# Reordering the start-up of a fused FFT and feed-forward kernel: splits ahead of the activation, a fold ahead of the copies, conversions one to three units earlier

## The chip, the cores and the metric

The kernel runs on one core of a Trainium2 chip. The metric is the device time of one execution in microseconds (us), the median over several runs. The kernel uses TensorE (PE, matrix products), VectorE (DVE), ScalarE (ACT), GpSimd (POOL) and the DMA queues, mostly SyncE's (SP).

## The reference, cut to what matters

```
X = np.fft.fft(np.fft.fft(x, axis=1), axis=2).real       # x: 8 x 3008 x 256, float32
h = X.reshape(24064, 256) @ w_in                          # w_in: 256 x 2048
g = np.where(h >= 1, h, np.where(h <= -1, 0, (h + 1) ** 2 / 4))
out = g @ w_out                                           # w_out: 2048 x 256
```

The weights arrive as 64-bit floats. The kernel turns them into float32 itself.

## The kernel before, in words

**Two kinds of work.** For each of the 8 batches the sequence transform is done as 64 x 47 (stage 1: eight pieces `p0` to `p7` per batch; then a small "nyquist" product `p8`; then stage 2: six pieces `p9` to `p14`, each of which makes half of one of three column chunks). The hidden-dimension transform is folded into `w_in`. What is left is cut into 384 *units*, one for each batch, column chunk `k` (three) and slice `f` of 128 of the 2048 hidden features. Batch 0 goes first through `f` 0 to 3 of the three chunks (units 0 to 11), then through `f` 4 to 15 of each (units 12 to 23, 24 to 35, 36 to 47).

**One unit.** `gemm1(i)` (L410) makes six products into two `uv` banks (three banks in all, L417), then DVE forms `us` (L422) and the two halves of `h` (L424, L425), then ACT makes `a` (Relu at L428, Square at L429). `activate(i)` (L432) joins `a` and `h` on DVE. For units under 24 the result `g` (L437) is multiplied in float32 (`wo32`, eight product records); from unit 24 on DVE's `h` (L440) is split by ACT into `gh` (L443) and by POOL into `gl` (L446), and `gemm2` makes twelve faster products. `gemm2` (L455) adds into four accumulator banks; at the end of a group of slices DVE and ACT empty two banks each (L489, L487; L485 where a stored part is added).

**The order of work at the start is written by hand.** `START` (L67) and `STEPS` (L72) name small steps by a letter and a number. In unit `i` of the main loop (L572) come, in this order: `gemm1(i)`, `activate(i-1)`, `gemm2` of an earlier unit, and then the steps of `STEPS[i]`. `gemm2` begins at unit 2, and is left out in the two units of `SKIP` (8 and 13), so that it then runs four units behind. `pin()` (L559) fixes each engine's order of issue to the program's order up to unit 23; after that the framework's scheduler orders. The steps that matter here:

- `a`, `b`, `c`, `d` of a weight block n convert it: `a` takes its fields (two DVE operations, L208 and L209), `b` is three on ACT (L214 to L216), `c` joins them (two on DVE, L221 and L222), `d` scales on POOL (L236; on DVE as `v`). Blocks 2, 3, 6, 7, 10, 11, 14 and 15 are parts of `w_out`, the others of `w_in`.
- `F`, `f` fold a half or a slice of `w_in` on PE and copy its high part on ACT (L279, L287); `s` makes its low part on DVE (L300, L305); `R`, `r`, `e`, `E` move a correction row `delta` (L291, L268).
- `u` and `O` make the high (ACT, L247) and low (DVE, L251) parts of `w_out` that units from 24 on need. The tile of the low parts lies on the raw blocks 6 to 9.
- `x`, `L` load the input of batch 0 and 1 (SP); `y`, `g` fold it (DVE or POOL, L137), and `Y` folds it on POOL behind DVE's last step.
- `p` issues the products of a piece; `t`, `w` copy stage 1 out of its bank (`w`: half on ACT at L339, half on DVE at L337); `q` splits a stage-2 piece into a high part on ACT (L174) and a low part on DVE (L175). `p8` also copies a row on ACT (L357) and stores it by a DMA from ACT's queue (L360); `n` (L367) waits for that store and reads it back over all partitions.
- `i`, `j` are products that only keep PE busy; `G` is `activate`.

**Banks.** The first 12 transform banks of batch 0 use the four accumulator banks in turn (L168). Those after share one bank, `fft`, so that `p12` must wait until `q11` has read `p11` out. Fold products 3 and 5 use a `uv` bank (L275).

**Later batches.** While a batch runs through its units, the next one's transform pieces are spread between them; for batch 1 this starts at unit `NEXT` = 23 (L575).

Of the kernel before, what the change touches and what calls it, by code (L numbers as in the profile page):

```python
# [26 lines left out]
NCHUNK = 3  # L27
NFT = FF // P
LAG = 4
SKIP = (8, 13)  # L30
EVICT_AHEAD = 150

C_ORDER = [*range(1, 8), 0, *range(8, NC)]
# [5 lines left out]
def _constants():  # L39
# [25 lines left out]


START = (  # L67
# [3 lines left out]
)  # L71
STEPS = {  # L72
    0: "p11 c2 d2 G0 i4",
    1: "q11 p12 a3 b3 i4",
    2: "a4 c3 d3 b4 q12",
    3: "c4 d4",
    4: "p13 a5 q13 b5",
    5: "p14 q14",
# [1 line left out]
    7: "a8 b8",  # L80
    8: "f2 f3 c8 d8 s2 s3 r1",
    9: "a9 b9",
    11: "a6 c9 d9 b6",
    12: "a12 b12",
    13: "f4 f5 c6 d6 s4 s5 r2",
    14: "a13 c12 d12",
    15: "b13",
    16: "a7 c13 d13 b7",
    17: "f6 c7 d7 s6 u0 L0 L1",
    18: "f7 a10 s7 b10 r3 u1",  # L90
    19: "a11 c10 d10 b11",
    20: "a14 O0 Y0 b14 u2 L2",
    21: "O1 c11 d11 u3",
    22: "a15 O2 Y1 b15 L3 u4",
    23: "O3 c14 d14 u5",
    24: "O4 c15 d15 u6",
    25: "O5 u7",
    26: "O6 O7",
}

RAW = {0: "gh", 1: "gh", 2: "woh", 3: "woh", 4: "woh", 5: "woh", 6: "wol", 7: "wol", 8: "wol", 9: "wol"}
# [6 lines left out]
NATIVE = 24  # L108
PINNED = 24
SPARE = (3, 5)  # L110
NEXT = 23


@with_exitstack
def fft_ffn_kernel(ctx: ExitStack, tc: tile.TileContext, x, cst, w_in, w_out, out):
# [16 lines left out]
    def fold_x(b, q, engine=None):  # L132

        t = xt.pop((b, q))
        engine = engine or nc.gpsimd
        y = sb.tile([96, CH], F32, tag="y", name=f"y_{b}_{q}", bufs=3)
        first = engine.tensor_tensor(y, t[:96, 0], t[:96, 1], op=ALU.add)  # L137
        yt[b, q] = y
        if q == 0:
            y = sb.tile([96, NA], F32, tag="yd", name=f"yd_{b}", bufs=1)  # L140
            engine.tensor_tensor(y, t[:96, 0, :NA], t[:96, 1, :NA], op=ALU.subtract)
            yt[b, "d"] = y
        return first.ins

    def fold_x_behind_vector(q):
        last = [ins for ins in traced if ins.engine == mybir.EngineType.DVE][-1]
        sync = mybir.DependencyInfo(mybir.DependencyClass.Sync, mybir.DependencyReason.DATA)
        tc.add_manual_dep(fold_x(1, q), last.name, sync, reason="beside VectorE's next steps")
# [158 lines left out]
    s1, s2 = {}, {}  # L307

    def stage1_sums(b, q):
        if q == 0:  # L310
            zt[b] = sb.tile([P, NC, P + 1], F32, tag="z", name=f"z_{b}", bufs=1)
        y = yt[b, q]
        bank = fft_bank(b, f"s1_{b}_{q}")
        pt = bank[:, : GPC * 96].rearrange("p (i n) -> p i n", i=GPC)
        for i in range(GPC):
            nc.tensor.matmul(pt[:, i], y[:, i * P : (i + 1) * P], bm[:96, :], start=True, stop=True)  # L316
        if q == 0:
            pd = bank[:NA, GPC * 96 : GPC * 96 + 2 * NC]
            nc.tensor.matmul(pd, yt[b, "d"], bm[:96, : 2 * NC], start=True, stop=True)
        s1[b, q] = bank  # L320
# [6 lines left out]
    def stage1_copy(b, q, vector=False):  # L327
        z, bank = zt[b], s1[b, q]
        if q == 0 and b:
            stage1_last(b, bank)  # L330
        pt = bank[:, : GPC * 96].rearrange("p (i n) -> p i n", i=GPC)
        for h in range(2):
            for m in range(2):
                src = pt[h * NA : (h + 1) * NA].rearrange("p i (t m c) -> p m c (i t)", t=2, m=2)[:, m]
                dst = z[m * NA : (m + 1) * NA, :, (2 * q + h) * 8 : (2 * q + h + 1) * 8]
                if vector and h:
                    ins = nc.vector.tensor_copy(dst, src)  # L337
                else:
                    ins = nc.scalar.activation(dst, src, AF.Copy)  # L339
                if b == 0:  # L340
                    if q:
                        tc.declare_no_dep(ins.ins, group="z", reason="other columns")
                    tc.add_to_no_dep_group("z", ins.ins)
    def stage1(b, q):
        for p in range(q, min(q + 2, XC)):
            if (b, p) in xt and (b, p) not in yt:
                fold_x(b, p)
        stage1_sums(b, q)
        stage1_copy(b, q)

# [43 lines left out]
    def fft_pieces(b):  # L394
        pieces = []
        for q in range(XC):
            pieces.append((4, lambda q=q: stage1(b, q)))
        pieces.append((2, lambda: nyquist(b)))
        for h in range(NC // 4):
            pieces.append((4, lambda h=h: stage2(b, h)))  # L400
        return pieces
# [8 lines left out]
    def gemm1(i):  # L410
        b, k, f = units[i]
        n = WIDTH[k]
        hi, lo = pq[b, k]
        cols = slice(f * P, (f + 1) * P)
        uv = []
        for m in range(2):
            t = ps.tile([P, CH], F32, tag="uv", name=f"uv_{i}_{m}", bufs=3)  # L417
            for j, (w, r) in enumerate(((wh, hi), (wl, hi), (wh, lo))):
                nc.tensor.matmul(t[:, :n], w[m][:, cols], r[:, m, :n], start=(j == 0), stop=(j == 2))  # L419
            uv.append(t[:, :n])  # L420
        us = sb.tile([P, CH], F32, tag="us", name=f"us_{i}", bufs=2)[:, :n]
        nc.vector.scalar_tensor_tensor(us, nyb[b, k][:, :n], delta[:, f : f + 1], uv[0], op0=ALU.mult, op1=ALU.add)  # L422
        h = sb.tile([P, 2, CH], F32, tag="h", name=f"h_{i}", bufs=3)[:, :, :n]
        nc.vector.tensor_tensor(h[:, 0], us, uv[1], op=ALU.subtract)  # L424
        nc.vector.tensor_tensor(h[:, 1], us, uv[1], op=ALU.add)  # L425
        a = sb.tile([P, 2, CH], F32, tag="a", name=f"a_{i}", bufs=3)[:, :, :n]

        nc.scalar.activation(a, h, AF.Relu, bias=half, scale=0.5)  # L428
        nc.scalar.activation(a, a, AF.Square)  # L429
        fronts[i] = h, a  # L430

    def activate(i):  # L432
        n = WIDTH[units[i][1]]
        h, a = fronts.pop(i)
        if i < NATIVE:
            g = sb.tile([P, 2, CH], F32, tag="gh", name=f"g_{i}", bufs=4)[:, :, :n]
            nc.vector.scalar_tensor_tensor(g, a, 1.0, h, op0=ALU.min, op1=ALU.max)  # L437
            acts[i] = (g,)
            return
        nc.vector.scalar_tensor_tensor(h, a, 1.0, h, op0=ALU.min, op1=ALU.max)  # L440
        gh = sb.tile([P, 2, CH], F32R, tag="gh", name=f"gh_{i}", bufs=4)[:, :, :n]
        gl = sb.tile([P, 2, CH], F32R, tag="gl", name=f"gl_{i}", bufs=4)[:, :, :n]
        nc.scalar.activation(gh, h, AF.Copy)  # L443
        acts[i] = gh, gl
        for sg in range(2):
            nc.gpsimd.tensor_tensor(gl[:, sg], h[:, sg], gh[:, sg].bitcast(F32), op=ALU.subtract)  # L446
# [61 lines left out]
    n1 = XC  # L508
# [43 lines left out]
    def run_steps(names):  # L552
        for s in names.split():
            steps[s[0]](int(s[1:] or 0))
# [17 lines left out]
    for i in range(n_units + LAG):  # L572
        if i < n_units:
            b, r = divmod(i, per)
            r0 = NEXT if b == 0 else 0  # L575
            if r == r0:
                pending = fft_pieces(b + 1) if b + 1 < NB else []
                done, total = 0, sum(w for w, _ in pending)
                if pending and b:
                    for q in range(4):  # L580
                        load_x(b + 1, q)
            gemm1(i)
            if b == 0 and units[i][2] == NFT - 2:
                load_parts(units[i][1])
            if 1 < i <= PINNED:
                activate(i - 1)
            if i >= PINNED:
                activate(i)
        first, _, then = STEPS.get(i, "").rpartition("|")
        run_steps(first)  # L590
        if 2 <= i < PINNED and i not in SKIP:
            gemm2(second)
# [72 lines left out]
```

## Time and profile before

| | |
|---|---|
| three runs | 1768.59, 1768.91 (median), 1779.52 us |
| the profiled execution's own time | 1767.59 us |
| its span | 1765.8 us |
| mean granted TensorE clock | 0.996 |
| PE busy | 1735.6 us (98%) |
| DVE busy | 1421.5 us (80%) |
| ACT busy | 1334.8 us (76%) |
| POOL busy | 1164.2 us (66%) |

The profile is of one execution. Each engine's instructions can be listed in order of time: start, duration, engine, source line, operation, output and input tiles, count, and in brackets how long the engine had been idle before it and what it waited for. Matmuls overlap at their ends, so a PE that looks busy can still lose a few tenths of a microsecond. A table of stages gives for each stretch the busy time of each engine, the granted clock (PEclk) and the DMA share.

### The profile page before, as it was taken

Reading aid. Unit: us, or ns where it says so; the run is one execution under the profiler, and the core shown is the slowest. Engines: PE = TensorE matmul, PEld = TensorE weight load, DVE = VectorE, ACT = ScalarE, POOL = GpSimd, SP = SyncE. Lnnn points to the kernel's source line nnn. Section 1 sums busy time; section 2 is a strip of 40 time slices with the busy share of each in tenths; the row PEclk is TensorE's granted clock in tenths of the full one; section 3 lists DMA queues with packets and bytes.
Section 4 is the critical chain, followed back from the end, with each engine's and each line's share of the span. In section 5 each row is a group of like instructions: output and inputs, shape, how many; then the busy total and the mean of one; then the engine's idle time right before and its main releaser. Section 6 shows DMA issues by size and latency. Waiting matters only on the chain.

```text
span 1765.8 us, 21536 instructions
## 1 busy us (share of the span) xinstructions
PE 1735.6 (98%) x7824; PEld 1394.4 (79%) x7824; DVE 1421.5 (80%) x1752; ACT 1334.8 (76%) x1558; POOL 1164.2 (66%) x807
## 2 busy tenths in 40 slices
PE   7998999999999999999999999999999999999998
PEld 5555788888888788888888888888888878888876
DVE  5898788888877888777878788878888788888886
ACT  5676777877777777777777877778778777777775
POOL 1113766876677766787667876677667766667766
PEclk8999999999999999999999999999999999999999
DMA  8023321111011100111001110111001001000000
GB/s 312 23 72 106 107 78 48 36 59 43 1 60 37 59 30 1 62 57 37 30 13 60 59 31 24 37 43 59 23 24 36 1 23 42 1 24 17 7 24 24
DMA packets 33737, 80.88 MB, mean 46 GB/s; under 512 B 4704, under 2 KB 9952, under 8 KB 33632
## 3 DMA queue, kind: packets, MB, share of 16 engines
q1 hardware_dynamic: 33596, 79.52, 13.2%
q8 instruction: 61, 1.00, 0.2%
q14 instruction: 44, 0.36, 0.1%
q10 hardware_dynamic: 36, 0.01, 0.0%
HBM read 51.70 MB, written 27.81 MB: 45 GB/s over the span
## 4 chain that ended last, share of the span: by engine, by line
PE 53%; ACT 15%; POOL 12%; DVE 10%; issue 9%; DMA 0%; ACTq 0%; POOLq 0%; SPq 0%; DVEq 0%
PE acc L478 33%; PE uv L419 16%; POOL gl L446 12%; DVE h L440 6%; ACT a L429 5%; ACT gh L443 4%; ACT a L428 4%; PE s L316 2%; PE s L382 1%; PE wps L279 1%; DVE h L424 1%; DVE h L425 1%; ACT z L339 1%; POOL y L137 0%; DVE us L422 0%
## 5 line engine op out<-in xcount | busy, mean ns | idle before, releaser
L446 POOL TENSOR_TENSOR gl<-h,gh 128x512 fp32r<-128x512 f32 (+1 forms) x720 | 1038.3, 1465 | 438.6 <-ACT gh L443 405.4
L440 DVE SCALAR_TENSOR_TENSOR h<-a,h 128x1024 f32<-128x1024 f32 (+1 forms) x360 | 543.1, 1509 | 219.8 <-ACT a L429 218.4
L443 ACT ACTIVATE gh<-h 128x1024 fp32r<-128x1024 f32 (+1 forms) x360 | 376.1, 1045 | 345.7 <-DVE h L440 301.5
L478 PE MATMUL acc<-gh,woh 128*128 128x512 f32 (+1 forms) x1440 | 570.5, 396 | 3.9 <-DVE o L489 2.5
L478 PE MATMUL acc<-gl,woh 128*128 128x512 f32 (+1 forms) x1440 | 563.9, 392 | 1.3 <-POOL gl L446 1.3
L478 PE MATMUL acc<-gh,wol 128*128 128x512 f32 (+1 forms) x1440 | 560.9, 390 | 0.0
L428 ACT ACTIVATE a<-h,biases 128x1024 f32<-128x1024 f32 (+1 forms) x384 | 431.7, 1124 | 44.5 <-DVE h L425 42.6
L429 ACT ACTIVATE a<-a 128x1024 f32<-128x1024 f32 (+1 forms) x384 | 398.9, 1039 | 7.7
L478 PEld LDWEIGHTS acc<-gh,woh 128*128 128x128 f32 x1440 | 270.7, 188 | 62.8 <-DVE o L489 5.9
L478 PEld LDWEIGHTS acc<-gl,woh 128*128 128x128 f32 x1440 | 271.3, 188 | 58.9 <-POOL gl L446 2.6
L478 PEld LDWEIGHTS acc<-gh,wol 128*128 128x128 f32 x1440 | 270.8, 188 | 54.7
L419 PE MATMUL uv<-pqh,wh 128*128 128x512 f32 (+1 forms) x768 | 310.7, 405 | 1.3 <-DVE h L425 1.0
L424 DVE TENSOR_TENSOR h<-us,uv 128x512 f32<-128x512 f32 (+1 forms) x384 | 259.7, 676 | 62.7 <-POOL gl L446 19.9
L422 DVE SCALAR_TENSOR_TENSOR us<-nyb,delta,uv 128x512 f32<-128x512 f32 (+1 forms) x384 | 279.1, 727 | 30.5 <-PE uv L419 29.9
L419 PE MATMUL uv<-pqh,wl 128*128 128x512 f32 (+1 forms) x768 | 299.6, 390 | 0.0
L419 PE MATMUL uv<-pql,wh 128*128 128x512 f32 (+1 forms) x768 | 299.2, 390 | 0.0
L425 DVE TENSOR_TENSOR h<-us,uv 128x512 f32<-128x512 f32 (+1 forms) x384 | 256.2, 667 | 0.0
L419 PEld LDWEIGHTS uv<-pqh,wh 128*128 128x128 f32 x768 | 144.6, 188 | 45.1 <-DVE h L425 6.7
L419 PEld LDWEIGHTS uv<-pqh,wl 128*128 128x128 f32 x768 | 144.5, 188 | 33.5 <-issue 5.3
L419 PEld LDWEIGHTS uv<-pql,wh 128*128 128x128 f32 x768 | 144.3, 188 | 30.4 <-issue 0.2
L137 POOL TENSOR_TENSOR y<-x 96x512 f32<-96x512 f32 x61 | 107.2, 1759 | 28.1 <-DMA x<-in_x_dram 10.2
L478 PE MATMUL acc<-g,wo 128*128 128x482 f32 (+1 forms) x192 | 85.9, 590 | 5.6 <-POOL wo L236 4.8
(64 smaller groups left out, 690.0 us busy)
## 6 DMA issues: line engine op xcount, KB each, us to landing
x<-in_x_dram SPq DMA_DIRECT2D x64, 512.0 KB, 3.5
out_dram<-o SPq DMA_DIRECT2D x26, 512.0 KB, 2.8
out_dram<-o SPq DMA_DIRECT2D x14, 482.0 KB, 2.9
nyb<-nyr SPq DMA_DIRECT2D x24, 256.0 KB, 3.3
raw<-in_moe_w_in_dram SPq DMA_DIRECT2D x4, 512.0 KB, 7.2
raw<-in_moe_w_out_dram SPq DMA_DIRECT2D x4, 512.0 KB, 11.5
part<-o SPq DMA_DIRECT2D x4, 512.0 KB, 3.1
os<-part SPq DMA_DIRECT2D x4, 512.0 KB, 4.3
```

What stands on the lines that cost most here:

```text
L137: first = engine.tensor_tensor(y, t[:96, 0], t[:96, 1], op=ALU.add)
L316: nc.tensor.matmul(pt[:, i], y[:, i * P : (i + 1) * P], bm[:96, :], start=True, stop=True)
L419: nc.tensor.matmul(t[:, :n], w[m][:, cols], r[:, m, :n], start=(j == 0), stop=(j == 2))
L422: nc.vector.scalar_tensor_tensor(us, nyb[b, k][:, :n], delta[:, f : f + 1], uv[0], op0=ALU.mult, op1=ALU.add)
L424: nc.vector.tensor_tensor(h[:, 0], us, uv[1], op=ALU.subtract)
L425: nc.vector.tensor_tensor(h[:, 1], us, uv[1], op=ALU.add)
L428: nc.scalar.activation(a, h, AF.Relu, bias=half, scale=0.5)
L429: nc.scalar.activation(a, a, AF.Square)
L440: nc.vector.scalar_tensor_tensor(h, a, 1.0, h, op0=ALU.min, op1=ALU.max)
L443: nc.scalar.activation(gh, h, AF.Copy)
L446: nc.gpsimd.tensor_tensor(gl[:, sg], h[:, sg], gh[:, sg].bitcast(F32), op=ALU.subtract)
L478: nc.tensor.matmul(acc[:, :n], w, g[:, sg], start=(begin and j == 0), stop=(last and j == len(terms) - 1))
```

## The change

In `START` the fold `y1` goes ahead of the first copies `w0`, and `p8` goes behind both; `y7` goes from behind `w4` to ahead of it. The sums and splits `p11`, `q11`, `p12` and `q12` leave `STEPS` (units 0 to 2) and are issued inside `gemm1`, the first two in unit 0 and the others in unit 1, after DVE's `h` and before ACT's `a`. From unit 10 on, conversions, folds, and the parts of `w_out` are issued one to three units earlier, the loads `L` and the fold `Y0` of batch 1 with them; the second skipped unit is 12 instead of 13, and batch 1's pieces start at unit 22. The first four input folds of batch 1 that `stage1` issues itself are tied behind DVE's last step as well.

```diff
-SKIP = (8, 13)
+SKIP = (8, 12)
...
-    "l0 l1 k m0 x0 x1 x2 x3 x4 x5 x6 x7 l2 l3 a0 b0 a1 b1 c0 v0 F0 F1 y0 p0 t0 j3 p8 c1 v1 w0 f0 y1 p1 g2 s0 f1 n0 "
-    "l4 l5 n1 n2 l8 l9 l6 l7 l12 l13 l10 l11 l14 l15 w1 s1 p2 g3 w2 p3 g4 w3 p4 g5 w4 p5 g6 y7 w5 j1 p6 j1 w6 p7 j2 w7 "
+    "l0 l1 k m0 x0 x1 x2 x3 x4 x5 x6 x7 l2 l3 a0 b0 a1 b1 c0 v0 F0 F1 y0 p0 t0 j3 c1 v1 y1 w0 p8 f0 p1 g2 s0 f1 n0 "
+    "l4 l5 n1 n2 l8 l9 l6 l7 l12 l13 l10 l11 l14 l15 w1 s1 p2 g3 w2 p3 g4 w3 p4 g5 y7 w4 p5 g6 w5 j1 p6 j1 w6 p7 j2 w7 "
     "a2 p9 p10 R0 q9 e0 q10 E0 b2"
 )
+AMID = {0: "p11 q11", 1: "p12 q12"}
 STEPS = {
-    0: "p11 c2 d2 G0 i4",
-    1: "q11 p12 a3 b3 i4",
-    2: "a4 c3 d3 b4 q12",
+    0: "c2 d2 G0 i4",
+    1: "a3 b3 i4",
+    2: "a4 c3 d3 b4",
...
-    11: "a6 c9 d9 b6",
-    12: "a12 b12",
-    13: "f4 f5 c6 d6 s4 s5 r2",
-    14: "a13 c12 d12",
-    15: "b13",
-    16: "a7 c13 d13 b7",
-    17: "f6 c7 d7 s6 u0 L0 L1",
-    18: "f7 a10 s7 b10 r3 u1",
-    19: "a11 c10 d10 b11",
-    20: "a14 O0 Y0 b14 u2 L2",
-    21: "O1 c11 d11 u3",
-    22: "a15 O2 Y1 b15 L3 u4",
-    23: "O3 c14 d14 u5",
-    24: "O4 c15 d15 u6",
-    25: "O5 u7",
-    26: "O6 O7",
+    10: "a6 c9 d9 b6",
+    11: "c6 d6",
+    12: "f4 f5 a12 s4 s5 b12 r2",
+    13: "a13 c12 d12 b13",
+    14: "a7 c13 d13 b7",
+    15: "c7 d7",
+    16: "f6 a10 s6 b10 L0 L1",
+    17: "f7 a11 c10 d10 s7 b11 r3 u0",
+    18: "O0 c11 d11 L2 u1",
+    19: "a14 O1 Y0 b14 L3",
+    20: "a15 c14 d14 b15 u2",
+    21: "O2 c15 d15 u3 u4",
+    22: "O3 O4 Y1 u5 u6",
+    23: "O5 O6 u7",
+    24: "O7",
 }
...
-NEXT = 23
+NEXT = 22
...
-                fold_x(b, p)
+                fold_x_behind_vector(p) if b == 1 and p < 4 else fold_x(b, p)
...
         a = sb.tile([P, 2, CH], F32, tag="a", name=f"a_{i}", bufs=3)[:, :, :n]
 
+        run_steps(AMID.get(i, ""))
         nc.scalar.activation(a, h, AF.Relu, bias=half, scale=0.5)
```

## The prediction

> **What bounds the kernel now.** I read the table of stages first, then PE's instructions in order of time with its idle gaps, then DVE's and ACT's around each gap.
>
> ```profile
> 0.00:215.00 215.00, 195.18 (x730) 124.19 (x731) 168.97 (x260) 144.90 (x208) 65.28 (x53) 0.97 0.36 125
> 215.00:500.00 285.00, 285.00 (x1340) 237.17 (x1339) 233.64 (x281) 219.19 (x254) 204.45 (x140) 1.00 0.13 45
> 34.00:45.00 11.00, 5.12 (x20) 4.91 (x21) 3.67 (x8) 4.55 (x6) 0.00 (x0) 0.54 0.49 183
> 80.00:125.00 45.00, 45.00 (x132) 24.49 (x131) 42.58 (x66) 34.80 (x45) 6.62 (x6) 1.00 0.21 71
> ```
>
> From 215 us on PE is never idle (285.00 of 285.00): a change that moves work can win nothing there. Nearly all that can be won is the 20 us that PE idles in the first 215, and the time it loses at a lower clock (0.54 between 34 and 45). Between 80 and 125 both PE (45.00) and DVE (42.58 of 45) are full, so a DVE step moved in there has little room.
>
> The gaps, on PE:
>
> ```profile
> 15.85 1.10 PE L316 MATMUL s<-cs,y 96*128 96x96 f32 x8 [2.15 <-DVE y L137]
> 31.94 0.38 PE L419 MATMUL uv<-pql,wh 128*128 128x482 f32 x1
> 39.88 2.04 PE L382 MATMUL s<-cs,z 128*128 128x128 f32 x8 [7.56 <-DVE pql L175]
> 41.72 1.92 PE L504 MATMUL warm_bank<-cs 128*128 128x128 f32 x8
> 58.76 1.05 PE L382 MATMUL s<-cs,z 128*128 128x128 f32 x8
> 59.57 0.48 PE L419 MATMUL uv<-pqh,wh 128*128 128x512 f32 x1
> 74.93 0.79 PE L419 MATMUL uv<-pqh,wh 128*128 128x512 f32 x1
> 84.58 0.80 PE L419 MATMUL uv<-pqh,wh 128*128 128x512 f32 x1
> 108.55 0.78 PE L419 MATMUL uv<-pqh,wh 128*128 128x482 f32 x1
> 139.26 5.20 PE L478 MATMUL acc<-g,wo 128*128 128x482 f32 x8 [2.04 <-POOL wo L236]
> 151.47 3.50 PE L478 MATMUL acc<-g,wo 128*128 128x482 f32 x8 [1.16 <-POOL wo L236]
> 164.10 1.08 PE L478 MATMUL acc<-g,wo 128*128 128x482 f32 x2 [1.64 <-POOL wo L236]
> ```
>
> **Part 1, the splits (the 7.56 us gap).** PE issued `p12` at 39.88 only because `q11`'s DVE half had not yet read the single `fft` bank. DVE and ACT show why it was so late:
>
> ```profile
> 30.05 0.65 DVE L425 TENSOR_TENSOR h<-us,uv 128x482 f32<-128x482 f32 x1
> 32.92 1.42 DVE L437 SCALAR_TENSOR_TENSOR g<-a,h 128x964 f32<-128x964 f32 x1 [1.01 <-ACT a L429]
> 35.64 0.65 DVE L425 TENSOR_TENSOR h<-us,uv 128x482 f32<-128x482 f32 x1
> 39.04 0.69 DVE L175 TENSOR_TENSOR pql<-s,pqh 128x512 fp32r<-128x512 f32 x1 [2.75 <-ACT pqh L174]
> 44.88 0.72 DVE L422 SCALAR_TENSOR_TENSOR us<-nyb,delta,uv 128x482 f32<-128x482 f32 x1 [4.47 <-PE uv L419]
> 54.15 1.16 DVE L437 SCALAR_TENSOR_TENSOR g<-a,h 128x964 f32<-128x964 f32 x1
> ```
>
> ```profile
> 29.02 0.72 ACT L216 ACTIVATE cv<-cv,biases 128x512 uint32<-128x512 f32 x1
> 37.52 1.01 ACT L429 ACTIVATE a<-a 128x964 f32<-128x964 f32 x1
> 38.43 0.58 ACT L174 ACTIVATE pqh<-s 128x512 fp32r<-128x512 f32 x1
> ```
>
> `q11`'s ACT half stood behind unit 1's activation (37.52 + 1.01), which waited for unit 1's `h` (35.64 + 0.65). Put ahead of unit 0's activation it waits for `p11` instead. `p11` is issued by PE before unit 1's products and ends near 30.1; ACT is free from 29.74 (29.02 + 0.72). So the ACT half runs from 30.1 to 30.7, just as DVE ends `h` (30.70), and behind it wait only unit 0's activation, which could not start earlier, and then `g_0` on DVE: the new wait costs nothing, but a late `p11` would delay both one for one. DVE's half ends at 31.4 and frees the bank; `p12` can follow unit 1's products at 32.2 instead of 39.88.
>
> What is late next is DVE.
>
> ```profile
> 32.05 1.27 POOL L236 TENSOR_TENSOR wo<-cv 128x512 f32<-128x512 f32 x1 [10.71 <-DVE cv L222]
> ```
>
> `c2` now ends 0.6 later, and `d2` on POOL runs from about 32.6 to 33.9, all beside `g_0`. In the profile `g_0` overlapped `d2` by 0.4 us (32.92 to 33.32) and took 1.42 instead of the 1.16 of a later one (54.15). I add 0.5: `g_0` ends at 34.9, `us_1` at 35.5, `h_1` at 36.75, then `q12`'s DVE half (0.6), `a3` (0.7), and `us_2` at 38.05 instead of 44.88. PE's second half of unit 2 waits for `us_1`'s bank, to 35.6. Carried on with the same durations, PE would begin unit 5's products at 49.9 (59.57 before) and unit 8's at 65.4 (74.93): a lead of **9.5 us**. As a check: the gap is 7.56, and the low clock stretched `p12` and the products behind it from 0.81 (58.76 to 59.57) to 1.84 (39.88 to 41.72), with the rest about 2.4 in all; 10.0 less some 0.5 of new short waits for `g_1`, `g_2`, `g_5`. Bounds: 7.5 (the clock stays low somewhere) and 10.2.
>
> The Trainium skill's page "TensorE: Matmul & The Clock Gate" (Part 1, "What's actually happening") says the clock drops to half after at least one idle window of about 3.4 us. The 7.56 gap agrees. The gap of 2.04 at 137.2 does not: the eight products after it took 5.20 where those at 151.47 took 3.50. By that rule the gap would have cost 2.04 alone, and the gain in the sum below would be 1.7 smaller.
>
> **Part 2, the fold and the copies at the start.** `p1` waited 2.15 us for `y1`, which stood on DVE behind the copies `w0`, and these behind ACT's:
>
> ```profile
> 12.93 0.56 ACTq L360 DMA_DIRECT2D nyr<-nyt  x1
> 13.54 0.68 ACT L339 ACTIVATE z<-s 64x192 f32<-64x192 f32 x2 [0.64 <-ACT nyt L357]
> 14.25 0.73 DVE L337 COPY z<-s 64x192 f32<-64x192 f32 x2 [2.67 <-ACT z L339]
> 15.02 0.69 DVE L137 TENSOR_TENSOR y<-x 96x512 f32<-96x512 f32 x1
> 17.99 0.34 SPq L367 DMA_DIRECT2D nyb<-nyr  x1
> ```
>
> With `y1` ahead and the row copy and ACT's DMA of `p8` behind, `w0` runs at about 12.0 to 13.5. But DVE's copies waited for ACT's (14.25) though they write other columns, so `p8`, which reads a column of the same tile, will probably wait for all four. PE then does `p8` at 13.5, the fold at 13.8, and `p1` at 14.65 instead of 15.85: **1.2 us**, which the chain `p1`, `g4`, `g6`, `p7`, `w7`, `p9` keeps. Bounds: 0 and 2.15. The DMA of the row leaves 1.2 later, so SP, with every weight load queued behind `n0`, goes on at 19.2 instead of 17.99. Of what is queued there, the row is needed first, by unit 0's `us` near 27.5, 8 us later, and the weight blocks behind it (4 and up) are first read after 40: nothing.
>
> **Part 3, the late conversions.** The three gaps of 2.04, 1.16 and 1.64 are `gemm2` of units 16, 18 and 20 waiting for `d10`, `d11`, `d14` on POOL, right behind `c10`, `c11`, `c14`. These are now made two, three and three units (near 4.6 us each) earlier, so the waits go even with PE 11 us ahead: 4.84, and 1.7 of low clock (5.20 - 3.50). **6.5 us**; bounds 4.8 and 7.0.
>
> **What that costs.** The moved steps land on DVE in units 10 to 18. Its prices and the eviction's:
>
> ```profile
> 115.38 1.07 ACT L487 ACTIVATE o<-acc 128x512 f32<-128x512 f32 x2
> ```
>
> ```profile
> 86.93 0.74 DVE L422 SCALAR_TENSOR_TENSOR us<-nyb,delta,uv 128x512 f32<-128x512 f32 x1
> 111.23 0.71 DVE L422 SCALAR_TENSOR_TENSOR us<-nyb,delta,uv 128x482 f32<-128x482 f32 x1
> 115.48 0.71 DVE L422 SCALAR_TENSOR_TENSOR us<-nyb,delta,uv 128x482 f32<-128x482 f32 x1
> 118.51 0.42 DVE L208 TENSOR_SCALAR cv<-raw_wol 128x512 uint32<-128x512 uint32 x1
> 119.18 0.68 DVE L221 SCALAR_TENSOR_TENSOR cv<-raw,cv 128x512 f32<-128x512 uint32 x1
> 120.39 0.71 DVE L422 SCALAR_TENSOR_TENSOR us<-nyb,delta,uv 128x482 f32<-128x482 f32 x1
> 160.92 1.77 DVE L222 SCALAR_TENSOR_TENSOR cv<-raw,cv 128x512 uint32<-128x512 uint32 x1
> ```
>
> A plain unit takes DVE 3.03 us (115.48 to 118.51), an `a` step 0.67, a `c` step 1.21; PE needs some 4.8 (84.58 to 108.55 for units 10 to 14). A unit with both an `a` and a `c` costs DVE 4.9, and unit 10, with an eviction of two banks too (1.07 on ACT at 115.38, about as much on DVE), 6.2. DVE's lag behind PE is 2.35 us at unit 10 (84.58 to 86.93) and was 2.7 at unit 15 (108.55 to 111.23). Added up, it now grows by 1.4 in unit 10 (6.2 of DVE against 4.8), shrinks by 0.5 in unit 11 and grows by 1.1 in unit 12, where DVE waits for the folds' ACT copies behind that unit's activation: 4.3 from unit 13 to 15. Two things on PE wait for it. Fold 5's `uv` bank comes free late and holds unit 14 up by 0.3. And in unit 16 `gemm2` needs the accumulators, which DVE and ACT empty only behind unit 15's `h` and activation: before, ACT began at 115.38, now some 1.6 later against PE, so PE waits about 1.5. Together **-1.8**; bounds 0 and -4. The units with the folds (16, 17) give the lag back. The work that DVE, ACT and POOL do is otherwise the same, only earlier; `NEXT` moves one transform piece from unit 24 or later to 22, PE work either way. The loads `L` go out where their buffers are free (`c12`, `c13`, `c10`, `c11` come first), and `Y` stays behind DVE's step.
>
> **Sum.** 1767.6 - 1.2 - 9.5 - 6.5 + 1.8 = 1752.2, against the profiled execution's own time. That lies 1.3 under the median of the runs, so I forecast **1752.5 us**. Own range 1747.5 to 1757.
>
> **The rivals.**
>
> *No wait takes the place of any removed one.* `p8` doesn't wait for `w0`, the accumulators are emptied in time: the bounds 2.15, 10.2, 7.0 and 0 give 1767.6 - 19.4 = 1748. For it: ACT is busy for only 34.80 of the 45 us from 80 to 125, so its half of the evictions has room. Against: DVE's 42.58 of 45.
>
> *DVE becomes the bound.* The lag reaches about 5.1 (the next unit's second `uv` bank is then still unread) and PE goes at DVE's pace, 4.9 to 5.5, through units 10 to 21: about 0.5 a unit for 11 units, 5.5 more, plus one half-clock stretch, 1.7: 1752.2 + 7.2 = 1759.4. For it: the same 42.58. Against: the folds in 16 and 17 add PE time, not DVE time.
>
> *The split buys little.* `p11` or the bank comes late and only the clock and half of the gap are won: 5 less, 1757; or the order of issue on ACT is not what the list says, and 9.5 goes entirely: 1762. For it: nothing but the closeness of 30.1 and 30.7.
>
> *Slower than before.* DVE and POOL shut each other out. At 160.92 a `c` operation took 1.77 instead of 0.68 beside a POOL operation. If the crowded conversions met POOL's `d` and folds in each unit from 10 to 23, 14 x 1.1 = 15.4, and three half-clock stretches 5.1, then 1.2 + 9.5 + 6.5 = 17.2 is won and 20.5 lost: 1771. It decides once the lag stands above 5.1 throughout. Against: a `d` mostly runs beside `us` and `h`, which showed no stretch, and `Y` and now the later folds are tied behind DVE. The skill's page "SBUF — State Buffer" ("Who interferes with whom") says the same: a DVE instruction with two SBUF inputs contends with a POOL instruction that reads SBUF. The trace agrees; by that rule too `us` and `h`, with one input in PSUM, escape.
>
> **How the numbers follow.** Forecast 0.61, no new wait 0.15, DVE the bound 0.15, split buys little 0.06, slower 0.03. A measurement of this kernel can tell about 1% from no change: under 1751.2 is faster. Of the forecast four in ten lies there, and all of the first rival: 0.24 + 0.15, rounded to 0.4. Slower by over 1% can only be the far part of the last rival: 0.02 at most. The range for 8 in 10 goes to the first two rivals and a little beyond: 1745 to 1761.
>
> **What would show it.** Right: `q11`'s ACT half near 29.5 (30.7 less the 1.2), no PE gap over 1 us between 30 and 45, clock 1.00 there, unit 8 at about 64 instead of 74.93, no wait for POOL's `wo`, a wait of 1 to 2 us for the eviction in unit 16. Wrong: a gap behind `h` or `g` in units 1 to 3, DVE never idle from unit 10 on with PE waiting at each `uv`, or a second clock drop.

## The result, and the profile after

The changed kernel took 1753.2 us (median of 4 runs, 1751.93 to 1754.1), the kernel before 1774.22 in the 4 runs beside it. The ratio is 0.9878, with a 95% interval of 0.9829 to 0.9926. The two profiled executions lie closer together: 1753.01 against 1767.59, which is 14.6 us or 0.8%. The prediction's sum was made against that second number. Why the medians differ by more is taken up at the run `b_fill` below. Here and below, the few executions that took 3% or more longer than the others of the same kernel are left out, among them the profiled one of `b_late` (2866.18 us, granted clock 0.555).

The table of stages of the kernel after (length, busy time of PE, PEld, DVE, ACT and POOL, granted clock, DMA share, GB/s):

```profile
30.00:45.00 15.00, 13.77 (x55) 8.60 (x54) 14.40 (x22) 11.05 (x15) 2.54 (x2) 1.00 0.63 239
0.00:200.00 200.00, 192.59 (x738) 122.58 (x739) 171.00 (x262) 144.98 (x208) 64.25 (x54) 1.00 0.39 137
200.00:500.00 300.00, 300.00 (x1407) 249.88 (x1406) 246.50 (x297) 233.09 (x272) 211.73 (x147) 1.00 0.14 46
```

PE idles 7.4 us in the first 200 (19.8 before), and it runs at full clock between 34 and 45, where the granted clock was 0.54 before. The list of what PE waited for in the first 215 us (total, times, longest) shows what is left. The three waits for POOL's `wo`, the 7.6 for `pql` and the 2.1 for `y` on DVE are gone; a wait of 1.9 for the emptied accumulators and one of 1.0 for `us` are new.

```profile
PE acc L479 <- DVE o L490: 1.9, 1, 1.9
PE s L316 <- ACT z L339: 1.7, 1, 1.7
...
PE uv L419 <- DVE us L422: 1.0, 1, 1.0
```

Lines of the new kernel stand one further on from the activation in `gemm1` on (in the edited kernels below by up to a few more): L429 and L430 are ACT's Relu and Square, L438 is DVE's `g`, L441 its `h`, L447 POOL's `gl`, L479 `gemm2`, L488 and L490 the evictions. PE in order of time, at the places that the prediction named:

```profile
13.43 1.06 PE L316 MATMUL s<-cs,y 96*128 96x96 f32 x8
...
23.01 2.02 PE L382 MATMUL s<-cs,z 128*128 128x128 f32 x16 [0.81 <-DVE z L337]
...
25.94 0.49 PE L419 MATMUL uv<-pqh,wh 128*128 128x482 f32 x1
...
30.54 1.05 PE L382 MATMUL s<-cs,z 128*128 128x128 f32 x8
...
32.24 0.47 PE L419 MATMUL uv<-pqh,wh 128*128 128x482 f32 x1
...
34.10 0.48 PE L419 MATMUL uv<-pqh,wh 128*128 128x482 f32 x1 [0.95 <-DVE us L422]
...
64.22 0.80 PE L419 MATMUL uv<-pqh,wh 128*128 128x512 f32 x1
...
106.54 3.58 PE L479 MATMUL acc<-g,wo 128*128 128x482 f32 x8 [1.88 <-DVE o L490]
...
166.45 0.77 PE L419 MATMUL uv<-pqh,wh 128*128 128x512 f32 x1
...
948.90 0.49 PE L419 MATMUL uv<-pqh,wh 128*128 128x482 f32 x1 [1.19 <-DVE h L425]
```

The row at 30.54 is `p12`, right behind unit 1's products, at full clock (1.05 instead of 2.04). The best yardstick for the rest is the time at which each unit's first product starts on PE:

| unit | before | after | lead |
|---|---|---|---|
| 0 | 27.57 | 25.94 | 1.63 |
| 2 | 43.28 | 32.24 | 11.04 |
| 8 | 74.93 | 64.22 | 10.71 |
| 13 | 99.07 | 88.35 | 10.72 |
| 14 | 103.81 | 93.61 | 10.20 |
| 16 | 113.29 | 102.79 | 10.50 |
| 17 | 118.17 | 111.27 | 6.90 |
| 21 | 143.74 | 131.20 | 12.54 |
| 28 | 182.50 | 166.45 | 16.05 |

1.63 comes from the start, 9.08 more from units 0 to 8 (9.41 of it is there at unit 2, before the new wait of 0.95). The lead sags at unit 17, by the wait of 1.88 and by a fold product that now stands one unit earlier, and grows by 5.34 between units 8 and 28, where the waits for `wo` used to be. At the end only 14.6 is left.

### The profile page after: what moved, and what is told of

Its sections match the earlier page's. It is cut to its first block, busy times and chain, and to the rows that moved or that the text cites. A ratio compares the mean times of both kernels' runs of the same rounds, so it can differ in the third digit from the quotient of the medians.

```text
span 1751.2 us, 21545 instructions
## 1 busy us (share of the span) xinstructions
PE 1732.2 (99%) x7824; PEld 1391.9 (79%) x7824; DVE 1424.2 (81%) x1752; ACT 1334.6 (76%) x1558; POOL 1160.0 (66%) x807
## 4 chain that ended last, share of the span: by engine, by line
PE 47%; ACT 20%; DVE 12%; POOL 11%; issue 9%; ACTq 0%; POOLq 0%; DVEq 0%
PE acc L479 29%; PE uv L419 14%; POOL gl L447 11%; DVE h L441 8%; ACT a L430 7%; ACT gh L444 6%; ACT a L429 5%; PE s L316 2%; PE s L382 1%; ACT z L339 1%; DVE h L424 1%; DVE h L425 1%; DVE g L438 1%; DVE us L422 0%; PE warm_bank L505 0%
## 5 line engine op out<-in xcount | busy, mean ns | idle before, releaser
L447 POOL TENSOR_TENSOR gl<-h,gh 128x512 fp32r<-128x512 f32 (+1 forms) x720 | 1036.2, 1462 | 445.8 <-ACT gh L444 409.6
L441 DVE SCALAR_TENSOR_TENSOR h<-a,h 128x1024 f32<-128x1024 f32 (+1 forms) x360 | 547.0, 1519 | 219.2 <-ACT a L430 217.7
L479 PE MATMUL acc<-gh,woh 128*128 128x512 f32 (+1 forms) x1440 | 570.2, 396 | 3.9 <-DVE o L490 2.5
L479 PE MATMUL acc<-gl,woh 128*128 128x512 f32 (+1 forms) x1440 | 563.9, 392 | 1.3 <-POOL gl L447 1.3
L479 PE MATMUL acc<-gh,wol 128*128 128x512 f32 (+1 forms) x1440 | 560.8, 389 | 0.0
L429 ACT ACTIVATE a<-h,biases 128x1024 f32<-128x1024 f32 (+1 forms) x384 | 431.5, 1124 | 31.5 <-DVE h L425 29.6
L430 ACT ACTIVATE a<-a 128x1024 f32<-128x1024 f32 (+1 forms) x384 | 399.0, 1039 | 7.7
L479 PEld LDWEIGHTS acc<-gh,woh 128*128 128x128 f32 x1440 | 270.7, 188 | 62.3 <-DVE o L490 5.9
L479 PEld LDWEIGHTS acc<-gl,woh 128*128 128x128 f32 x1440 | 271.3, 188 | 59.0 <-POOL gl L447 2.6
L479 PEld LDWEIGHTS acc<-gh,wol 128*128 128x128 f32 x1440 | 270.7, 188 | 54.8
L479 PE MATMUL acc<-g,wo 128*128 128x482 f32 (+1 forms) x192 | 83.7, 578 | 2.4 <-DVE o L490 1.9
```

Of the source, the lines that this page charges most:

```text
L479: nc.tensor.matmul(acc[:, :n], w, g[:, sg], start=(begin and j == 0), stop=(last and j == len(terms) - 1))
```

## The experiments

**The splits alone** (`b_splits`: the kernel before, with this part only).

```diff
+AMID = {0: "p11 q11", 1: "p12 q12"}
-    0: "p11 c2 d2 G0 i4",
-    1: "q11 p12 a3 b3 i4",
-    2: "a4 c3 d3 b4 q12",
+    0: "c2 d2 G0 i4",
+    1: "a3 b3 i4",
+    2: "a4 c3 d3 b4",
...
+        run_steps(AMID.get(i, ""))
```

> The kernel before with the splits alone moved ahead of the activation. Theory (each part takes away its own gaps on PE): the 7.56 us gap and the low clock behind it go, a wait near 1 us for us_1 comes in their place, PE begins unit 8 about 9.0 us earlier than 74.93, and the whole is 8 to 10 us faster; the three waits for POOL's wo stay. Rival (the gain is shared, PE stalls again later without the other parts): under 6 us.

1764.68 us, ratio 0.9955 (0.9935 to 0.9975); the profiled execution took 1760.61, 7.0 less than that of the kernel before, where 8 to 10 were expected. PE in order of time:

```profile
29.07 0.49 PE L420 MATMUL uv<-pqh,wh 128*128 128x482 f32 x1
...
37.29 0.48 PE L420 MATMUL uv<-pqh,wh 128*128 128x482 f32 x1 [1.02 <-DVE us L423]
...
67.42 0.80 PE L420 MATMUL uv<-pqh,wh 128*128 128x512 f32 x1
...
131.71 5.20 PE L480 MATMUL acc<-g,wo 128*128 128x482 f32 x8 [2.05 <-POOL wo L237]
```

From unit 0 to unit 8 pass 38.35 us (67.42 - 29.07) against 47.36 before: 9.0 by this part alone, with the same wait for `us` as in the whole change. Unit 0 itself came 1.5 later than before because this execution ran at half clock for 3.41 us behind the 2.15 gap, which has nothing to do with the edit; without that the 7.0 would be near 8.5, by estimate. The waits for `wo` are still all there.

**The start alone** (`b_start`: the kernel before with the new `START`).

```diff
-... p8 c1 v1 w0 f0 y1 p1 ... g5 w4 p5 g6 y7 w5 ...
+... c1 v1 y1 w0 p8 f0 p1 ... g5 y7 w4 p5 g6 w5 ...
```

> The kernel before with the new START list alone. Theory: p1 starts near 13.4 instead of 15.85, unit 0 about 1.6 us earlier, and since the chain behind the 7.56 us gap starts from unit 0, the gap moves with it: 1.2 to 2 us faster. Rival (the gap swallows it): 0, the gap near 9 us.

1766.14 us, ratio 0.9966 (0.9952 to 0.998). PE's gap before `p12` stays, and so does the low clock at it:

```profile
38.21 2.05 PE L382 MATMUL s<-cs,z 128*128 128x128 f32 x8 [7.51 <-DVE pql L175]
...
73.61 0.80 PE L419 MATMUL uv<-pqh,wh 128*128 128x512 f32 x1
```

`p12` comes 1.67 earlier than before (39.88), unit 8 1.3 earlier. So the start is worth 1.3 to 1.7, and the gains of the two parts add up. The 12 runs lie within 3 us (1765.12 to 1768.12), those of the kernel before beside it between 1767.29 and 1782.54.

**The late part alone** (`b_late`, and the same kernel as `b_late2`): the kernel before with only this part, the steps from unit 10 on as in the change's diff.

```diff
-SKIP = (8, 13)
+SKIP = (8, 12)
...
-NEXT = 23
+NEXT = 22
...
-                fold_x(b, p)
+                fold_x_behind_vector(p) if b == 1 and p < 4 else fold_x(b, p)
```

> The kernel before with the late conversions, the second skipped unit, NEXT and the tied folds alone. Theory: the three waits for POOL's wo (4.84) and the low clock behind the first (1.7) go, against a wait of 1.5 to 2 us for the eviction in unit 16 and 0.5 at unit 14: 4 to 5 us faster. Rival (the eviction's wait comes only from the earlier start): 6.5 faster. Rival (DVE is the bound from unit 10 on): 2 or less.

1770.06 us, ratio 0.9978 (0.9959 to 0.9998). That is 1.4 less than the kernel before beside it (1771.46), where 4 to 5 were expected; both kernels have the gap of 2.15 at the start, and the runs of both scatter by 9 us and more. Its schedule is read from one more execution of the same kernel, `b_late2`.

> The kernel before with the late part alone, once more for a trace at full clock. Theory: no wait for POOL's wo, unit 24 4 to 5 us earlier than 160.56 of which the extra transform piece ahead of it hides 0.9, a wait of 1.5 to 2 us for the eviction in unit 16.

1764.42 us for that one execution (before: 1767.59 in its profiled one). PE around unit 16 in it:

```profile
117.74 3.59 PE L477 MATMUL acc<-g,wo 128*128 128x482 f32 x8 [1.90 <-DVE o L488]
```

No wait for `wo` is left, and unit 28 starts at 177.65, 4.85 earlier than before. Counted from unit 8, ahead of the edit (75.39, against 74.93), it is 5.31, as in the whole change (5.34). The wait for the eviction is here in full (1.90) though PE runs eleven microseconds later than in the whole change: it comes with the late part itself, not from PE being early.

**The change without its late part** (`a_nolate`: the changed kernel, with the steps from unit 10 on as in the kernel before).

```diff
-SKIP = (8, 12)
+SKIP = (8, 13)
...
-NEXT = 22
+NEXT = 23
...
-                fold_x_behind_vector(p) if b == 1 and p < 4 else fold_x(b, p)
+                fold_x(b, p)
```

> The changed kernel with the late part (STEPS from 10 on, the skipped unit, NEXT, the tied folds) as before; the splits and the start stay changed. Theory (the parts' gains add up): the three waits for POOL's wo are back (4.8 us, with up to 1.7 of low clock), the eviction's wait of 1.88 in unit 16 is gone: 3.5 to 5 us slower than the changed kernel. Rival (the late part is worth nothing once the rest is in): within 1 us of it.

1757.21 us, ratio 0.9916 (0.989 to 0.9943). PE in order of time:

```profile
128.59 3.50 PE L480 MATMUL acc<-g,wo 128*128 128x482 f32 x8 [2.05 <-POOL wo L237]
...
139.11 3.50 PE L480 MATMUL acc<-g,wo 128*128 128x482 f32 x8 [1.16 <-POOL wo L237]
...
151.72 1.07 PE L480 MATMUL acc<-g,wo 128*128 128x482 f32 x2 [1.63 <-POOL wo L237]
```

The three waits are back with the same lengths, PE being ahead or not: POOL's `wo` was always late by its place in the list. 4.0 us slower than the change by the medians (2.2 against the change's second set of runs, `a_again` below), 3.1 by the profiled executions. In this execution the 2.05 gap brought no low clock (3.50 behind it, not 5.20); with it the difference would be about 4.8.

**What the low clock is worth** (`b_warm`, `b_fill`: products that only keep PE busy, put into the gaps of the kernel before).

```diff
-    1: "q11 p12 a3 b3 i4",
+    1: "i34 q11 p12 a3 b3 i4",
```

> The kernel before with 34 extra products on PE between unit 1's products and p12, that is, in the 7.56 us gap; nothing else is moved. Theory (the gap costs its length and the low clock after it): p12 still starts near 39.9, the clock stays at 1.00, p12 and the products behind it take 0.8 each instead of 1.84 and 1.56, and the whole is 2 to 2.6 us faster. Rival (the clock stretch is hidden by DVE, whose chain sets unit 2): 0.

1769.67 us, ratio 0.9985 (0.9966 to 1.0003). The table of stages of its profiled execution, which took 1780.03:

```profile
16.00:43.00 27.00, 26.99 (x113) 25.04 (x113) 12.29 (x26) 10.85 (x24) 4.25 (x4) 0.50 0.87 309
43.00:60.00 17.00, 17.00 (x113) 14.62 (x113) 9.54 (x15) 8.07 (x11) 1.01 (x2) 1.00 0.01 1
```

The filler kept PE busy (26.99 of 27.00 us), and yet this execution was slower, because the clock had already halved behind the *other* gap, that of 2.15 us before `p1`, and stayed so for 27 us. So a second kernel fills that gap too:

```diff
-... w0 f0 y1 p1 ...
+... w0 f0 i9 y1 p1 ...
-    1: "q11 p12 a3 b3 i4",
+    1: "i34 q11 p12 a3 b3 i4",
```

> The kernel before with 34 extra products on PE in the 7.56 us gap and 9 in the 2.15 us gap ahead of p1; nothing is moved. Theory (the kernel's spread between 1767 and 1782 us is time at half clock that gaps in the first 40 us set off): mean granted clock 0.997 or more in every run, all times between 1765 and 1770. Rival (the spread has another source): times over 1774 at a clock of 0.991 as often as before.

1765.39 us, ratio 0.9963 (0.9947 to 0.9979), with a granted clock of 0.998 or more in its runs. The same stretch of it:

```profile
16.00:43.00 27.00, 26.48 (x208) 24.95 (x209) 17.19 (x34) 15.75 (x30) 5.04 (x4) 1.00 0.83 306
```

No wait is removed here; PE has the same work to do and only does more on top. From unit 0 (27.72) to unit 8 (72.69) pass 44.97 us instead of 47.36: the low clock at the 7.56 gap cost 2.39. The runs also bear on the medians: of the 17 runs of the kernel before beside it, those at a mean clock of 0.995 to 0.996 took 1767.5 to 1771.4, and those at 0.988 to 0.991 took 1776 to 1778. With the 2.15 gap filled (`b_fill`) or gone (`b_start`) none of 24 runs took 1770 us. So the kernel before sometimes pays a long half-clock stretch at this gap, of the kind that `b_warm` shows (no trace of such a run of the kernel before itself was kept). The changed kernel has no such gap at the start, and its 4 runs lie within 2.2 us.

**The wait for the accumulators** (`a_c13`: the changed kernel, one conversion a unit later).

```diff
-    14: "a7 c13 d13 b7",
-    15: "c7 d7",
+    14: "a7 b7",
+    15: "c13 d13 c7 d7",
```

> The changed kernel with c13 and d13 moved from unit 14 to unit 15, ahead of c7, which is behind the eviction. Theory (the 1.88 us wait in unit 16 is DVE's lag, so it shrinks by a c step of 1.2): wait 0.6 to 0.8, 1 to 1.3 us faster than the changed kernel. Rival (the wait is set by ACT's half of the eviction): unchanged. Rival (the fold of unit 16 then waits for d13): the gain is given back there.

1754.0 us, ratio 0.9894 (0.987 to 0.9919). PE in order of time, with ACT at the second place (first of the changed kernel, then of this one):

```profile
105.65 3.80 PE L479 MATMUL acc<-g,wo 128*128 128x482 f32 x8 [0.69 <-DVE o L490]
...
146.52 1.10 PE L316 MATMUL s<-cs,y 96*128 96x96 f32 x8 [0.51 <-issue]
```

```profile
144.20 1.39 ACT L339 ACTIVATE z<-s 64x192 f32<-64x192 f32 x4
```

```profile
145.04 1.39 ACT L339 ACTIVATE z<-s 64x192 f32<-64x192 f32 x4
```

The wait falls from 1.88 to 0.69: it does come from DVE's conversions ahead of the eviction. But PE gets nothing for it. At 146.52 the next transform piece starts as late as in the changed kernel, where it starts at 146.51 without a wait. It stands right behind ACT's copies, which free its bank (145.04 + 1.39 = 146.43); in the changed kernel they ended at 145.59. What came in between shows on DVE behind the eviction (of the changed kernel, then DVE and POOL of this one):

```profile
107.51 0.68 DVE L222 SCALAR_TENSOR_TENSOR cv<-raw_wol,cv 128x512 uint32<-128x512 uint32 x1
```

```profile
107.82 1.75 DVE L222 SCALAR_TENSOR_TENSOR cv<-raw_wol,cv 128x512 uint32<-128x512 uint32 x1
```

```profile
107.47 1.56 POOL L236 TENSOR_TENSOR cv<-cv 128x512 f32<-128x512 f32 x1 [7.82 <-DVE cv L222]
```

The moved `d13` on POOL now meets `c7` on DVE, which takes 1.07 longer, and `c13` itself stands there too: unit 16's `us` starts at 109.50 instead of 108.11, and by unit 23 DVE and ACT are still 0.85 later than in the changed kernel. PE, which had begun unit 0 0.27 later than in the changed kernel, was 0.66 ahead of it at unit 17 (110.61 against 111.27), and at unit 24 it is 0.08 behind (147.41 against 147.33). So nothing is won.

**The wait for `us` in unit 2** (`a_d2`: POOL's `d2` is tied behind DVE's `g_0`).

```diff
-    0: "c2 d2 G0 i4",
+    0: "c2 G0 D2 i4",
...
+    def scale_behind_vector(n):
+        last = [ins for ins in traced if ins.engine == mybir.EngineType.DVE][-1]
...
+        tc.add_manual_dep(convert_scale(n, nc.gpsimd), last.name, sync, reason="behind VectorE's last step")
```

> The changed kernel with d2 on POOL tied behind g_0 on DVE, so that they no longer meet. Theory (g_0 took 2.12 instead of 1.16 because POOL's operation held the shared way to SBUF): g_0 takes about 1.2, the 0.95 us gap on PE in unit 2 goes, 0.7 to 1.1 us faster. Rival (g_0 is slow for another reason): 2.12 again, no difference. Rival (unit 0's second product then waits for wo): a new gap of 1 us or more ahead of the first gemm2.

1751.92 us, ratio 0.9887 (0.986 to 0.9913). First DVE and POOL of the changed kernel, then DVE, POOL and PE of this one:

```profile
31.30 2.12 DVE L438 SCALAR_TENSOR_TENSOR g<-a,h 128x964 f32<-128x964 f32 x1 [0.25 <-ACT a L430]
```

```profile
31.13 1.27 POOL L236 TENSOR_TENSOR wo<-cv 128x512 f32<-128x512 f32 x1 [11.70 <-DVE cv L222]
```

```profile
31.46 1.17 DVE L443 SCALAR_TENSOR_TENSOR g<-a,h 128x964 f32<-128x964 f32 x1 [0.26 <-ACT a L435]
```

```profile
32.70 1.29 POOL L236 TENSOR_TENSOR wo<-cv 128x512 f32<-128x512 f32 x1 [13.14 <-DVE g L443]
```

```profile
33.31 0.48 PE L424 MATMUL uv<-pqh,wh 128*128 128x482 f32 x1
```

`g_0` takes 1.17 instead of 2.12, the wait of 0.95 on PE is gone, and unit 8 starts 0.76 earlier (63.46). With 1.10 us of POOL's operation beside it, one DVE operation had lost 0.95. In the whole time the gain is not shown: 1751.92 lies at the lower end of the changed kernel's runs (1751.93 to 1754.1), and this kernel's own go from 1750.76 to 1754.23.

**The changed kernel once more, and both edits** (`a_again`, unedited, so without a diff; `a_both`, the two diffs of `a_d2` and `a_c13` together).

> The changed kernel once more, unedited, as the neighbour on this chip for the two kernels beside it and as a second trace. Theory (the 1.19 us gap near 949 us, where POOL and DVE hold each other up, follows from the order of issue): it is there again. Rival (it is a matter of moments): it is gone or elsewhere, and the whole is about 1 us faster for it.

> The changed kernel with d2 tied behind g_0 and c13 d13 moved to unit 15, both. Theory from the two alone (d2 wins 0.8 to 1.0, c13 wins 1.2 at unit 16 and gives it back at unit 23, where a transform piece waits for ACT's copies): 0.7 to 1.1 us faster than the changed kernel at unit 24, no more than with d2 alone. Rival (with PE 0.8 us earlier both hold): 1.8 to 2.1.

1754.98 us, ratio 0.9904 (0.9882 to 0.9926), and 1753.5 us, ratio 0.9891 (0.9869 to 0.9912). The changed kernel's second execution has no gap near 949, so that one was a matter of moments. But its wait for the eviction set off the low clock:

```profile
106.69 5.28 PE L479 MATMUL acc<-g,wo 128*128 128x482 f32 x8 [1.90 <-DVE o L490]
```

```profile
106.00:114.00 8.00, 7.30 (x15) 3.39 (x16) 5.94 (x10) 4.37 (x7) 1.27 (x1) 0.79 0.70 247
```

The same eight products took 3.58 in the first execution, 1.7 us less. The two medians differ by 1.8, but that this is the reason is not shown: the profiled execution of `a_y7` below paid the same. With both edits the wait is 0.68 with no low clock behind it in the profiled execution, and unit 24 starts at 146.24, 1.1 before the changed kernel's 147.33. The time is no better than with `d2` moved alone; here a wait of 1.64 for ACT's copies, at 181.14, was followed by half clock.

**The fold `y7` back in its place** (`a_y7`: the changed kernel, `y7` again behind `w4` and `g6`).

```diff
-... g5 y7 w4 p5 g6 w5 ...
+... g5 w4 p5 g6 y7 w5 ...
```

> The changed kernel with y7 back behind g6, where it stood before. Theory (y7 on DVE took 1.52 instead of 0.69 beside POOL's fold, pushed the last copies back, and so made the 0.81 us wait of p9): y7 takes about 0.7, p9's wait falls to 0.5 or less and unit 0 begins 0.3 to 0.5 us earlier. Rival (p7 then waits for y7): unit 0 no earlier or later.

1752.53 us, ratio 0.9887 (0.9867 to 0.9907). DVE of the changed kernel, then DVE and PE of this one:

```profile
18.45 1.52 DVE L137 TENSOR_TENSOR y<-x 96x512 f32<-96x512 f32 x1
```

```profile
19.31 0.69 DVE L137 TENSOR_TENSOR y<-x 96x512 f32<-96x512 f32 x1
```

```profile
22.29 2.02 PE L382 MATMUL s<-cs,z 128*128 128x128 f32 x16 [0.53 <-DVE z L337]
...
25.22 0.49 PE L419 MATMUL uv<-pqh,wh 128*128 128x482 f32 x1
```

Moved ahead, `y7` meets POOL's `g6` (18.16 to 19.42) and takes 1.52; left where it was it takes 0.69, and `p9` and unit 0 come 0.72 earlier. So this one move in `START` was a small loss: about 0.7 at unit 0. Unit 28 is 1.1 later than in the first execution all the same, since here too the eviction's wait was followed by half clock (5.28). The kernel's runs (1749.51 to 1754.15) lie below those of `a_again` beside it (1753.65 to 1757.12) but for an overlap of half a microsecond; against the change's first four runs they show no difference. No version is shown to beat the changed kernel.

## Why the prediction was right

The time came out at 1753.2 where 1752.5 was forecast, and each part can be held against its own term.

**The splits, 9.5 foreseen, 9.1 measured.** The mechanism is as described: with 1.63 added, `p12`'s 30.54 is the 32.2 foreseen. `q11`'s ACT half ran at 28.52 and `p12` stood right behind unit 1 (ACT and DVE of the changed kernel):

```profile
28.52 0.60 ACT L174 ACTIVATE pqh<-s 128x512 fp32r<-128x512 f32 x1 [0.42 <-PE s L382]
29.12 1.10 ACT L429 ACTIVATE a<-h,biases 128x964 f32<-128x964 f32 x1
```

```profile
29.15 0.69 DVE L175 TENSOR_TENSOR pql<-s,pqh 128x512 fp32r<-128x512 f32 x1
```

ACT's half ended at 29.12, just as `h` did on DVE, which is the meeting that was foreseen (30.7 for both, moved by the start). The 29.5 that the prediction names is that end, not the beginning, and it came 0.4 sooner because the start won that much more. The term that was too small is the stretch of `g_0`: 0.5 was added for its meeting with `d2`, by a row in which they overlapped for 0.4 us. They now overlapped for 1.1 us (31.30 to 32.40) and the stretch was 0.96.

**The start, 1.2 foreseen, 1.63 measured, by a wrong step.** The prediction held that `p8` would probably wait for all four copies `w0`. It did not: the nyquist products and their copy were done before DVE's copies began (PE, ACT and DVE of the changed kernel).

```profile
12.22 0.31 PE L355 MATMUL ny<-cs,z 128*24 128x64 f32 x2
```

```profile
12.62 0.21 ACT L357 ACTIVATE nyt<-ny 24x64 f32<-24x64 f32 x1
```

```profile
11.48 1.75 DVE L137 TENSOR_TENSOR y<-x 96x512 f32<-96x512 f32 x1
13.27 0.74 DVE L337 COPY z<-s 64x192 f32<-64x192 f32 x2
```

`p1` came at 13.43 instead of the 14.65 of the sum: 2.4 won there, above the bound of 2.15; 0.12 of it stands on PE before the first edited step already (the fold at 8.33 instead of 8.45). The row's DMA left at 12.86, no later than before (12.93). Of the 2.4, 0.8 was lost on the way to unit 0, most of it to `y7`, as `a_y7` shows (0.72). Two errors of opposite sign nearly met.

**The late part, 6.5 less 1.8 foreseen, 5.3 measured, in the whole change and alone.** All three waits for `wo` went. The sum for DVE is borne out step by step: its lag behind PE, from a unit's first product to its `us`, was to grow by 1.4 in unit 10, shrink by 0.5 in unit 11, grow by 1.1 in unit 12 and then stand at 4.3. It grew by 1.42, shrank by 0.50, grew by 1.25, and was 4.50, 4.17 and 4.63 in units 13 to 15. The wait for the eviction in unit 16 was 1.88 (1.5 foreseen), and 0.52 was lost at unit 14 (0.3 foreseen): 5.26 passed between units 13 and 14 against 4.74 in `a_nolate`; 0.30 of it came back by unit 15. That would leave 4.4; but between units 8 and 28 PE's busy time fell by 2.4 (102.73 to 100.35 by the table of stages), 0.9 more than the low clock and unit 14 account for. That rest is not traced to an instruction.

The sum put nothing for a low clock behind the new wait. The first execution had none; `a_again` and `a_y7` had one, at 1.7 us. So it is luck, worth 1.7 us, that 1753.01 came so near the forecast. That the eviction waits for DVE's conversions is shown by `a_c13`. That taking most of the wait away brings nothing is shown there too, and was not foreseen: the moved steps met on DVE and POOL, and ACT's copies came 0.84 later behind them.

**The tail.** "From 215 us on ... a change that moves work can win nothing there" held, but something was lost. PE's lead was 16.05 at unit 28, 15.75 at unit 32 (203.98 and 188.23), and 14.6 at the end; by the starts of the units it falls from 16.55 at unit 192 to 15.14 at unit 208, across the gap of 1.19 at 948.90. The gap does not belong to the edits as such: in `a_again` it is absent, and there the lead falls elsewhere (by 0.84 between units 96 and 112, where PE shows no gap of 0.3). The schedule from unit 24 on is not pinned. From unit 28 to the last unit the two executions of the changed kernel lost 1.5 and 1.7, those of its edited versions 1.3 to 3.9, in different places; what decides where was not tried. At 949 DVE's `h` was long, beside POOL's `gl` (DVE and POOL of the changed kernel, then of `a_again`):

```profile
945.69 2.59 DVE L441 SCALAR_TENSOR_TENSOR h<-a,h 128x964 f32<-128x964 f32 x1 [1.19 <-ACT a L430]
944.84 2.42 POOL L447 TENSOR_TENSOR gl<-h,gh 128x482 fp32r<-128x482 f32 x2
```

```profile
944.48 1.40 DVE L441 SCALAR_TENSOR_TENSOR h<-a,h 128x964 f32<-128x964 f32 x1 [0.92 <-ACT a L430]
943.62 3.35 POOL L447 TENSOR_TENSOR gl<-h,gh 128x482 fp32r<-128x482 f32 x2 [2.50 <-ACT gh L444]
```

In both, `h` meets two `gl`. In the first execution it was DVE's operation that grew longer for it, in the second one of POOL's.

**The rivals.** "No new wait" falls by the two waits of 0.95 and 1.88; "the split buys little" by `b_splits`. "DVE becomes the bound" falls too: from unit 8 to unit 16 pass 38.57 us, against 38.36 before, and from 8 to 28 fewer than before, so DVE did not set PE's pace there, but for the two waits named. The rival on the slower side, DVE and POOL shutting each other out, is real as a mechanism, but it was seen at `g_0`, `y1`, `y7` and near 949 (and at `c7` in `a_c13`), not in each unit. Whether the gain is over 1% hangs on which executions of the kernel before one compares with: 0.8% by the profiled ones, 1.2% by the medians, which by `b_fill` and `b_start` hold its long stretches of low clock. The prediction's sum had only the profiled one to go by.

## What to carry to other kernels

An instruction that only frees a buffer belongs ahead of one that waits for something else; to find such a pair, take the longest wait of the bounding engine and look at what stands before its releaser in that engine's order. Before a wait is removed, look for what would be late next: here 1.2 us of a wait was taken out in unit 16, and PE had nothing of it left by unit 24, because the step that was moved for it met another engine's. Where two engines share a resource, price a meeting by how long the two overlap in the new order, not by a row in which they barely touched.

## What the runs showed of the hardware

**Short gaps halve the clock, but not each time.** Gaps of 1.45 to 2.15 us on PE were followed by half clock in some executions of the same instructions and not in others. The eight products behind the 2.05 wait for `wo` took 5.20 in `b_splits` and 3.50 in `a_nolate`; those behind the wait for the eviction 3.58 in the first execution of the changed kernel and 5.28 in the second. The stretches at half clock in the trace's record are 3.41 us long, or 10.24 (at the gap of 7.5 to 7.6, in three executions), or 27.31 (in `b_warm`, behind 2.15): one, three and eight times the same length. The Trainium skill's page "TensorE: Matmul & The Clock Gate" (Part 1, "What's actually happening") gives a free-running window of 3413 ns, which fits these lengths; that it takes at least one idle window does not fit the gaps of 1.45 to 2.15.

**Where the gap falls decides in part.** In each trace the clock changes only at instants that lie whole multiples of 3.413 us apart. All traces but `b_late`'s hold 33 gaps of 1.4 to 2.2 us on PE. Twelve were followed by half clock, and each of these lay, but for 0.13 us at most, between two neighbouring instants. Thirteen were cut by an instant into parts of 0.45 us or more, and none of these was followed by it. The other eight lay between two instants as well, or nearly so, and were not followed by it, so this is not the whole rule. The wait for the eviction was cut in the first execution of the changed kernel (0.69 and 1.19), and in `a_again` it was not.

**A busy PE did not get its clock back.** In `b_warm` PE was busy for 26.99 of 27.00 us and the clock stayed at 0.50 throughout. Why this stretch was eight windows long and the others mostly one is open.

**DVE beside POOL.** Three DVE operations of the changed kernel with both inputs in SBUF ran 0.8 to 1.1 us longer beside a POOL operation: 2.12 against 1.17 (`g_0`), 1.52 against 0.69 (`y7`), 1.75 against 0.69 (`y1`, whose row of before is 0.69). `g_0` and `y7` lost 0.96 and 0.83 in overlaps of 1.1 and 0.97 (18.45 to 19.42): nearly all of the time that they shared. The Trainium skill's page "SBUF — State Buffer" ("Who interferes with whom") says that such a pair shuts each other out, and these rows agree. Which of the two loses is not fixed: near 949 `h` took 2.59 and the two `gl` beside it 2.42 in one execution, 1.40 and 3.35 in the other.
